# A verdict moved into the last products, and a linear attention plus gated MLP kernel's order table written anew

## The chip, the cores and the metric

The kernel runs on one core of one Trainium2 chip. The metric is device time in microseconds (us) of one execution; less is better. The core has five engines with a queue of instructions each, and every queue is executed in its own order: PE (matrix products), DVE (vector), ACT (scalar), POOL (GpSimd) and SP, which here only issues DMA transfers. Each instruction may wait on semaphores that other engines or transfers raise.

## What is computed

First a linear attention with a decaying state, for 4 batches, 8 heads, 768 positions and head size 48, then a gated MLP on the 3072 tokens with 384 features and 1536 hidden features:

```python
for t in range(S):
    state = alpha[:, :, t, :, None] * state + np.einsum('bhd,bhe->bhde', k[:, :, t], v[:, :, t])
    y[:, :, t] = np.einsum('bhd,bhde->bhe', q[:, :, t], state)
...
x = np.ascontiguousarray(attn_out.transpose(0, 2, 1, 3)).reshape(B * S, H * D)
g = x @ w_gate
silu = g * (1.0 / (1.0 + np.exp(-g)))
val = x @ w_val
return (silu * val @ w_out).astype(np.float32)
```

q, k, v and alpha are float32; the three weights come as 64-bit floats, and the kernel cuts their bits down to 32 itself.

## The kernel before

**Attention.** The positions of all batches are cut into 16 units u of 192. For each unit DVE makes two scans over the decays (`backward`, line 459, and `forward`, line 468), and q and k are multiplied by the results. PE makes the scores (`scores`, line 553), the state that is carried on (`carry`, lines 593 and 603) and the outputs (`outputs`, lines 658 to 675); DVE masks the scores (`causal`, line 613). The output rows are split into a high and a low part (`rows_hi` on ACT, line 689; `rows_lo` on DVE, line 693) and stored as columns of `xT`. In units 0 to 3 the inputs are turned by PE: `widened` copies an input to a padded tile (line 402), `pe_transposed` turns it (line 414), and a copy takes it out of PSUM (line 833). Later units are turned by DVE (line 394).

**MLP.** Tokens are worked on in 8 blocks of 384, hidden features in 12 pieces of 128: 96 steps. A step s has a gate product g and a value product v (`product`, line 748, nine matmuls each, three split products for each third of the features), ACT's silu (line 756), DVE's product `hidden` (line 760), the split of the hidden tile into a high part (`hidden_hi`, ACT, line 764) and a low part (`hidden_lo`, line 769, on DVE or POOL), and the out product o (`out_product`, line 780, nine matmuls into three PSUM banks). At the end of a block `out_rows` (line 792) takes the three banks out and `out_store` (line 797) stores them. The first block can start once units 0 and 1 are through. The g and the v product have one PSUM bank each, so v of the next step waits until `hidden` has read the one before.

**Weights.** Twenty groups of one or two pieces are loaded while the first steps run; each is cut from 64 to 32 bits in three operations (lines 156 to 174) and split in two (lines 340 and 344), shared among ACT, DVE and POOL.

**Range checks.** The fast path is right only where the weights and alpha lie in fixed ranges. So all weights and alpha are loaded once more (`range_load`, `alpha_load`) into three buffers and checked on ACT (lines 316 to 318 for each of 36 weight pieces, lines 453 and 454 for each of 16 alpha pieces), which leaves sums in `viol` and `wviol`. At the very end these are reduced on DVE, compared and multiplied, PE sums over the partitions (line 954), DVE writes `flag` (line 955), every engine loads `flag` into a register (line 1106) and branches on it (line 1107): past the slow general path where all is in range.

**The order.** `ORDER` is a text of some 1500 words that fixes, by hand, the order of nearly all instructions. A word such as `v:G0` or `t:S5@01` names an engine (t PE, v DVE, s ACT, g POOL, y SP), a task, and for PE the PSUM banks by number. The program takes the words in turn, each engine gets its instructions in that order, and the framework adds the semaphores. What stands behind the loop over `ORDER`, the reduction of the checks among it, was placed by the framework's own scheduler:

```python
for word in ORDER.split():
    e, name = word.split(":")
    name, *banks = name.split("@")
    todo.pop(name)(engines[e], *(BANKS[int(x)] for x in "".join(banks)))
```

Names in `ORDER`: `La0 Lq0 Lk0` load a unit's inputs, `pa0` widens alpha of unit 0, `Ta0` turns it, `ea0` takes it out, `G0 f0` are the scans, `S0 Bw0 B4 Y0` scores, carry and outputs, `ma` the mask, `yh yl` the split of output rows, `R x` and `xr` the way into `xT`; `w4v0 w4v1 w4v2 w4a w4p` are the five operations on weight group 4; `g3 v3 sl3 h3 hh3 hl3 o3 ot3 os3` belong to step 3; `wr wc` and `Lc ck` are loads and checks of the ranges.

Of the kernel before, what the change touches and what calls it, by code (L numbers as in the profile page):

```python
# [46 lines left out]
y:La0 s:pa0 y:wl0 t:Ta0@73 y:La1 s:ea0 y:Lq0 s:pa1 y:Lk0 v:w0v0 v:w0v1 v:w0v2 v:G0 t:Ta1@50 s:pq0 s:w0a y:Lq1 y:Lk1  # L47
v:f0 s:pk0 t:Tq0@36 t:Tk0@47 g:z0 g:pq1 v:q0 v:mk0 s:pk1 s:ea1 s:qc0 y:La2 t:Tk1@30 s:ek1 t:K0.2@4 y:Lk2 s:kc0.2
t:K0.0@1 v:G1 y:V0 s:kc0.0 t:Tq1@36 y:wl1 s:pa2 t:S0@05 v:mk1 g:w0p t:K0.1@7 t:K1.1@4 s:cq1 s:vc0 y:wl3 y:Lq2 s:kc0.1
y:wl2 v:f1 v:ma0.1 s:w1v0 v:ma0.0 g:q1 s:w3v0 t:Ta2@26 s:qc1 s:ea2 t:Bw0@7 s:ad0.2 v:z1 v:ma0.2 v:w1v1 v:w3v1 v:w1v2  # L50
s:ad0.1 y:V1 s:kc1.1 v:G2 t:K1.2@5 t:S1@16 g:w1a t:K1.0@2 v:de1 v:ma1.1 v:ma1.0 v:ma1.2 t:Y0@70 v:f2 y:La3 s:kc1.0
v:w3v2 s:kc1.2 v:z2 y:wl6 s:pa3 t:Bw1@4 s:yh0.0 s:w2v0 g:w1p t:Ta3@56 y:wl4 s:vc1 v:yl0.0 s:ad1.1 s:yh0.1 g:pk2
t:Y1@23 g:pq2 v:w2v1 y:V2 s:ad1.2 v:w2v2 s:w4v0 s:yh1.0 t:Tk2@41 s:w2a s:yh1.1 v:yl0.1 t:R0.1@0 v:mk2 t:Tq2@74 v:q2
t:R0.0@1 t:K2.0@7 v:yl1.0 y:Lk3 t:R0.2@4 s:x0.0 s:ea3 v:yl1.1 g:w3a s:kc2.0 y:Lq3 s:x0.2 s:pq3 v:x0.1 y:wl9 t:K2.2@2
t:R1.2@5 t:R1.0@6 t:R1.1@0 v:de2 t:K2.1@4 s:x1.1 v:w4v1 s:x1.0 g:w3p y:wl5 g:pk3 y:wl14 y:V3 t:Tk3@13 y:wl10 s:x1.2
g:w2p t:Tq3@70 v:G3 v:ad0.0 t:g0 s:kc2.1 v:w4v2 v:f3 s:kc2.2 s:cq3 s:w6v0 t:v0 s:w5v0 s:vc2 t:S2@70 v:w5v1 y:wl7 s:qc2
t:Bw2@2 s:sl0 s:w4a y:wl13 v:w5v2 g:q3 t:g1 g:w4p s:ad2.1 v:ma2.2 v:h0 y:La4 v:ma2.0 s:sl1 s:ad2.2 s:w5a t:v1 v:mk3
v:ma2.1 y:wl8 t:K3.1@4 v:de3 t:K3.0@1 s:kc3.1 v:w6v1 s:kc3.0 t:Y2@27 y:wl11 y:Lk4 s:yh2.0 s:hh0 t:S3@41 g:hl0 s:w7v0
v:w5p v:w6v2 t:Bw3@3 t:g2 v:ma3.2 v:h1 s:yh2.1 s:hh1 v:yl2.0 v:ma3.1 v:w7v1 v:w7v2 y:wl12 g:qc3 s:sl2 s:w9v0 g:w6a
s:ad3.1 t:v2 s:vc3 v:hl1 s:w7a v:ma3.0 t:g3 s:sl3 v:yl2.1 t:o0 t:Y3@01 v:h2 v:w7p g:w6p s:w8v0 t:K3.2@2 s:w10v0 v:w9v1  # L60
v:w9v2 s:hh2 g:z3 v:w8v1 v:w8v2 s:w8a v:w10v1 s:yh3.0 t:v3 v:h3 t:g4 t:o1 y:xr2 v:yl3.0 v:w8p g:hl2 t:v4 s:w9a s:sl4
t:o2 s:hh3 v:w10v2 s:yh3.1 g:hl3 t:g5 v:yl3.1 v:h4 s:w11v0 t:o3 v:w9p t:v5 s:w10a g:w10p s:w12v0 v:tr4 s:hh4 v:w11v1
v:w11v2 s:sl5 v:h5 t:g6 v:w12v1 v:w12v2 s:w14v0 t:v6 g:hl4 s:hh5 v:tk4 t:o4 s:w11a g:w11p y:xr3 s:sl6 t:g7 v:h6 v:G4
s:hh6 s:kc3.2 s:w12a s:w13v0 t:v7 g:hl5 y:Lq4 s:sl7 v:mk4 y:wl16 t:o5 v:w12p v:h7 t:g8 v:f4 g:hl6 g:z4 s:sl8 t:v8 t:g9
v:w14v1 s:hh7 v:hl7 y:wl15 v:w14v2 v:h8 s:sl9 t:o6 v:ot6.2 v:tq4 s:ot6.0 y:wl18 t:v9 s:hh8 t:g10 v:h9 v:w13v1 g:hl8
s:w15v0 t:v10 v:w15v1 y:os6.0 v:q4 g:qc4 s:sl10 v:w15v2 s:ot6.1 t:g11 v:w13v2 y:La5 s:w13a t:o7 s:hh9 v:h10 y:os6.1
# [1072 lines left out]
```

## Time and profile before

| what | value |
|---|---|
| time, three executions | 564.78 us median (563.24 to 565.94) |
| time of the profiled execution | 563.72 us |
| span of its trace, first to last instruction | 562.0 us |
| granted TensorE clock over the span, mean | 0.993 |
| busy: DVE | 387.3 us (69%) |
| busy: ACT | 277.5 us (49%) |
| busy: POOL | 158.2 us (28%) |
| DMA | 77.64 MB, mean 138 GB/s |

The profiled execution lies 1.06 us below the median of the three. The span is shorter than the time by 1.72 us, which lie around the program. A row of a timeline gives the start in us from the span's start, the time of the group, the engine, the line, the operation, output and input tiles by name, the shape, the number of instructions, and in brackets how long the engine stood idle before it and what ended that.

### The profile page before, as it was taken

What the parts mean: (1) busy time and instruction counts of PE and PEld (TensorE: products, weight loads), DVE (VectorE), ACT (ScalarE), POOL (GpSimd) and SP (SyncE); (2) the same over time, 40 slices, a digit from 0 to 9 for tenths busy, and PEclk for the clock granted to TensorE, in tenths of its full rate; (3) what the DMA queues carried; (4) which work ended last, traced back from release to release, by engine and by line L of the source; (5) the groups of instructions that cost most, each with busy time, mean ns of one, the idle gap of its engine ahead of it and who ended that gap; (6) DMA issues with size and microseconds to landing.
All of it is one profiled execution on the core that took longest, in us unless ns stands there. A gap on an engine that the chain in (4) does not pass through costs nothing.

```text
span 562.0 us, 13554 instructions
## 1 busy us (share of the span) xinstructions
PE 538.6 (96%) x5398; PEld 522.4 (93%) x5398; DVE 387.3 (69%) x599; ACT 277.5 (49%) x616; POOL 158.2 (28%) x159
## 2 busy tenths in 40 slices
PE   4899999998999999999999999999999999999992
PEld 4789899998899999999999999999999999999992
DVE  7999999979997888879879887754683403121121
ACT  6987653443123213244562453556666464546452
...
GB/s 244 271 240 261 203 170 164 176 103 114 135 146 156 98 153 155 118 106 183 77 163 141 150 90 182 157 87 170 188 138 58 71 109 146 71 77 106 22 77 48
DMA packets 95366, 77.64 MB, mean 138 GB/s; under 512 B 32832, under 2 KB 92224, under 8 KB 95296
## 3 DMA queue, kind: packets, MB, share of 16 engines
...
HBM read 62.52 MB, written 5.90 MB: 122 GB/s over the span
## 4 chain that ended last, share of the span: by engine, by line
PE 84%; DVE 10%; issue 2%; ACT 1%; DMA 1%; POOL 0%; ACTq 0%; DVEq 0%
PE ops L780 26%; PE g L748 25%; PE v L748 25%; PE y L675 2%; PE A L603 2%; PE s L553 2%; DVE Gs L459 2%; PE y L658 1%; DVE t L164 1%; DVE t L174 1%; DVE X L613 1%; PE y L659 1%; DVE V L642 1%; DVE AT L468 1%; DMA Le<-in_alpha_dram 1%
## 5 line engine op out<-in xcount | busy, mean ns | idle before, releaser
L748 PE MATMUL v<-xT,w 128*128 128x384 f32 x864 | 166.6, 336 | 1.4 <-DVE h L760 1.4
L748 PE MATMUL g<-xT,w 128*128 128x384 f32 x864 | 166.8, 337 | 0.0
L780 PE MATMUL ops<-w,hh 128*128 128x384 f32 x576 | 160.9, 337 | 0.8 <-DVE X L613 0.8
L769 POOL TENSOR_TENSOR hl<-h,hh 128x384 fp32r<-128x384 f32 x63 | 74.2, 1179 | 291.2 <-ACT hh L764 291.1
L748 PEld LDWEIGHTS v<-xT,w 128*128 128x128 f32 x864 | 150.6, 188 | 2.6 <-DVE h L760 2.0
L748 PEld LDWEIGHTS g<-xT,w 128*128 128x128 f32 x864 | 150.4, 188 | 0.8
L760 DVE TENSOR_TENSOR h<-h,v 128x384 f32<-128x384 f32 x96 | 53.0, 552 | 112.6 <-PE v L748 97.1
L756 ACT ACTIVATE h<-g 128x384 f32<-128x384 f32 x96 | 47.0, 490 | 125.7 <-PE g L748 119.1
L780 PEld LDWEIGHTS ops<-w,hh 128*128 128x128 f32 x576 | 105.8, 188 | 1.7 <-DVE X L613 1.2
L780 PE MATMUL ops<-w,hl 128*128 128x384 f32 x288 | 96.9, 336 | 0.0
L764 ACT CAST hh<-h 128x384 fp32r<-128x384 f32 x96 | 48.8, 510 | 97.1 <-PE ops L780 60.3
L528 DVE STREAM_TRANSPOSE K<-Gs 32x384 f32<-32x384 f32 x96 | 54.7, 570 | 1.9
L780 PEld LDWEIGHTS ops<-w,hl 128*128 128x128 f32 x288 | 54.1, 188 | 0.0
L769 DVE TENSOR_TENSOR hl<-h,hh 128x384 fp32r<-128x384 f32 x33 | 21.5, 650 | 21.0 <-ACT hh L764 20.8
L468 DVE TENSOR_TENSOR_SCAN AT<-AT,back 128x771 f32<-128x771 f32 x16 | 29.5, 1846 | 0.6
L459 DVE TENSOR_TENSOR_SCAN Gs<-AT,inj 128x772 f32<-128x772 f32 x16 | 29.2, 1823 | 0.3 <-ACT AT L833 0.2
L613 DVE TENSOR_TENSOR X<-s,mask 64x384 f32<-64x384 f32 (+1 forms) x48 | 26.4, 552 | 2.0 <-PE s L553 1.2
L487 POOL TENSOR_TENSOR X<-trq,AT 112x768 f32<-112x768 f32 x10 | 17.9, 1786 | 35.2 <-DMA L<-in_k_dram 11.6
L344 POOL TENSOR_TENSOR w<-t,w 128x768 fp32r<-128x768 f32 (+1 forms) x14 | 25.5, 1824 | 3.7 <-ACT w L340 3.3
L174 DVE SCALAR_TENSOR_TENSOR t<-raw,t 128x768 uint32<-128x768 uint32 (+1 forms) x20 | 24.4, 1229 | 0.3
L317 ACT ACTIVATE wc<-wc,wbias 128x384 f32<-128x384 f32 x36 | 23.5, 653 | 1.2
L318 ACT ACTIVATE wc<-wc,wbias 128x384 f32<-128x384 f32 x36 | 23.4, 650 | 1.2
...
## 6 DMA issues: line engine op xcount, KB each, us to landing
...
```

The costliest lines, as they stand in the source:

```text
L174: eng.scalar_tensor_tensor(out=t, in0=hi, scalar=0x3FFFFFFF, in1=t, op0=ALU.bitwise_or, op1=ALU.bitwise_and)
L344: eng.tensor_tensor(out=lo, in0=src, in1=hi.bitcast(F32), op=ALU.subtract)
L459: nc.vector.tensor_tensor_scan(*(x.rearrange("p g t -> p (g t)")[:, ::-1] for x in (Gs, AT, inj)), 0.0, op0=ALU.mult, op1=ALU.add)
L468: nc.vector.tensor_tensor_scan(Af, Af, back[:, 1 : n + 1], back[:, 0:1], op0=ALU.mult, op1=ALU.add)
L528: nc.vector.transpose(out=bass.AP(k0.tensor, k0.offset, [k0.ap[0], (G * 2 * D, NU), (2 * D, G), (1, 32)]), in_=Kg[j * BO + x : j * BO + x ...
L613: nc.vector.tensor_tensor(out=X[r, z, f * GF : (f + 1) * GF, :].rearrange("r g (c t) -> r g c t", c=NU), in0=sps[f][r].rearrange("r g (c t ...
L748: nc.tensor.matmul(pt, wsp[kind, f][a][:, kt * P : (kt + 1) * P], xT[blk][:, b_, kt, :], start=(n == 0), stop=(n == 3 * KT - 1),)
L756: nc.scalar.activation(h, acc.pop(("g", blk, f)), AF.Silu)
L760: nc.vector.tensor_tensor(out=h, in0=h, in1=acc.pop(("v", blk, f)), op=ALU.mult)
L764: nc.scalar.copy(out=hh, in_=acc["h", blk, f])
L769: eng.tensor_tensor(out=hl, in0=acc.pop(("h", blk, f)), in1=hh.bitcast(F32), op=ALU.subtract)
L780: nc.tensor.matmul(ops[blk][i], h[b_][:, i * P : (i + 1) * P], wsp["o", f][a], start=(first and n == 0), stop=(last and n == 2),)
```

## The change

Three things are changed, and no arithmetic.

1. The reduction of the checks is no longer behind the loop. It is two tasks, `fa` (DVE: reduce, compare, multiply, and a memset of ones) and `fb` (PE's sum and DVE's write of `flag`), with places in `ORDER` among the last products.
2. `ORDER` is a new text: tasks stand elsewhere, some are on another engine, and PE's tasks have other banks. By count of tasks, 24 `hl` went from POOL to DVE and 22 from DVE to POOL, 4 q products went from DVE to POOL and 2 back, 3 k products from POOL to DVE and 1 back, 4 low weight parts from DVE to POOL and 3 back, 5 `ot` from ACT to DVE and 4 back. The widening of alpha of unit 0 goes from ACT to POOL.
3. The checks of the ranges are begun earlier and none is left for the end: 19 of 52 stand ahead of the gate product of step 48, where there were 8.

```diff
 ORDER = """
...
-t:o94 y:os83.1 t:o95 v:ot95.0 s:ck13 s:ot95.2 y:os95.0 v:ot95.1 y:os95.1 s:os95.2 v:z15 s:ck15
...
 """
...
+    checks = {}
+
+    def checks_joined(eng):
+
+        oks = []
+        for nm, t_, most in (("a", viol, 0.0), ("w", wviol[:, 0, :], 0.0), ("s", wviol[:, 1, :], W_SUM)):
+            vs = cp.tile([P, 1], F32, name="vs" + nm)
+            nc.vector.tensor_reduce(vs, t_, axis=AX.X, op=ALU.add)
+            okf = cp.tile([P, 1], F32, name="ok" + nm)
+            nc.vector.tensor_scalar(out=okf, in0=vs, scalar1=most, scalar2=None, op0=ALU.is_le)
+            oks.append(okf)
+        okf = oks[0]
+        for t_ in oks[1:]:
+            nc.vector.tensor_tensor(out=okf, in0=okf, in1=t_, op=ALU.mult)
+        ones = cp.tile([P, 1], F32, name="ones")
+        nc.vector.memset(ones, 1.0)
+        checks.update(ones=ones, okf=okf)
+
+    def verdict(eng):
+
+        cps = ps.tile([1, 1], F32, tag="A2", name="cps")
+        nc.tensor.matmul(cps, checks["ones"], checks["okf"], start=True, stop=True)
+        nc.vector.tensor_copy(out=flag, in_=cps)
+
+    todo["fa"] = checks_joined
+    todo["fb"] = verdict
...
-    oks = []
-    for nm, t_, most in (("a", viol, 0.0), ("w", wviol[:, 0, :], 0.0), ("s", wviol[:, 1, :], W_SUM)):
...
-    ones = cp.tile([P, 1], F32, name="ones")
-    nc.vector.memset(ones, 1.0)
-    cps = ps.tile([1, 1], F32, tag="A2", name="cps")
-    nc.tensor.matmul(cps, ones, okf, start=True, stop=True)
-    nc.vector.tensor_copy(out=flag, in_=cps)
```

The end of the new text reads `v:fa v:h95 t:o93 t:fb g:hl94 s:hh95 v:hl95 t:o94 y:os83.2 t:o95 s:ot95.0 s:ot95.1 s:ot95.2 y:os95.0 s:os95.2 y:os95.1`. The table shows little by itself; three places show what it makes of the queues. Line numbers of the changed kernel are lower by 89, since the text of `ORDER` has fewer lines.

**The end, on ACT and DVE.** `ac` is a piece of alpha under check, `ot` an output tile, `hh` a high part, `vs` and `ok` the sums and verdicts of the checks. ACT's last rows before:

```order
L764 CAST hh_11_6734<-h_11_6697 128x384
L453 ACTIVATE ac_6730<-ac_6730,nbias 128x576
L454 ACTIVATE ac_6730,viol<-ac_6730,dbias 128x576
L792 COPY ot_2_11_6763<-ops_2_0_6389 128x384
L797 DMA out_dram<-ot_2_11_6763 128x384
L453 ACTIVATE ac_6695<-ac_6695,nbias 128x576
L454 ACTIVATE ac_6695,viol<-ac_6695,dbias 128x576
L1106 TENSOR_LOAD flag
```

and now:

```order
L675 CAST hh_11_6760<-h_11_6725 128x384
L703 COPY ot_0_11_6783<-ops_0_0_6386 128x384
L703 COPY ot_1_11_6785<-ops_1_0_6387 128x384
L703 COPY ot_2_11_6787<-ops_2_0_6388 128x384
L708 DMA out_dram<-ot_2_11_6787 128x384
L1027 TENSOR_LOAD flag
```

DVE's last rows before:

```order
L769 TENSOR_TENSOR hl_11_6738<-h_11_6697,hh_11_6734 128x384
L792 COPY ot_0_11_6759<-ops_0_0_6387 128x384
L792 COPY ot_1_11_6766<-ops_1_0_6388 128x384
L472 MEMSET AT 128x3
L944 TENSOR_REDUCE vsa<-viol 128x1
L946 TENSOR_SCALAR oka<-vsa 128x1
L950 TENSOR_TENSOR oka<-oka,okw 128x1
L950 TENSOR_TENSOR oka<-oka,oks 128x1
L955 CAST flag<-cps 1x1
L1106 TENSOR_LOAD flag
```

Ahead of these, elsewhere on DVE, the scheduler had put the two sums over the weights, `vsw` and `vss`. Now:

```order
L671 TENSOR_TENSOR h_10_6700<-h_10_6700,v_10_6683 128x384
L850 TENSOR_REDUCE vsa<-viol 128x1
L852 TENSOR_SCALAR oka<-vsa 128x1
L850 TENSOR_REDUCE vsw<-wviol 128x1
L852 TENSOR_SCALAR okw<-vsw 128x1
L850 TENSOR_REDUCE vss<-wviol 128x1
L852 TENSOR_SCALAR oks<-vss 128x1
L856 TENSOR_TENSOR oka<-oka,okw 128x1
L856 TENSOR_TENSOR oka<-oka,oks 128x1
L858 MEMSET ones 128x1
L671 TENSOR_TENSOR h_11_6725<-h_11_6725,v_11_6713 128x384
L865 CAST flag<-cps 1x1
```

Two alpha checks leave ACT's end, the three output copies are all on ACT now, and the write of `flag` stands ahead of DVE's last `hl`, which is one row further on, followed by the load of `flag`. On PE the sum `cps` stands between the out products of steps 93 and 94. On SP the load of `flag` stands ahead of its last two stores.

**The beginning, on POOL and DVE.** `wide` is the padded tile for PE's turning, `Le` alpha of unit 0, `sel` and `K` constants, `raw` and `t` a weight piece before and after it is cut. POOL before:

```order
L242 AFFINE_SELECT mask<-mask 64x64 x2
L266 COPY K_105<-ident 48x4x48 x2
L371 CAST sel_121<-ident 48x48 x2
L371 CAST sel_122<-ident 48x48 x2
L472 MEMSET AT 128x3
```

and now:

```order
L153 AFFINE_SELECT mask<-mask 64x64 x2
L313 COPY wide<-Le 128x12x48
L177 COPY K_105<-ident 48x4x48 x2
L282 CAST sel_121<-ident 48x48 x2
L282 CAST sel_122<-ident 48x48 x2
L383 MEMSET AT 128x3
```

DVE before, from behind its memsets (a scan is printed as SCALAR_TENSOR_TENSOR with `Gs<-AT,inj` or `AT<-AT,back`):

```order
L158 TENSOR_SCALAR t_149<-raw_133 128x384
L168 SCALAR_TENSOR_TENSOR t_149<-raw_133,t_149 128x384
L174 SCALAR_TENSOR_TENSOR t_149<-raw_133,t_149 128x384
L459 SCALAR_TENSOR_TENSOR Gs_153<-AT,inj 128x772
L465 RECIPROCAL back<-Gs_153 128x4
L468 SCALAR_TENSOR_TENSOR AT<-AT,back 128x771
```

and now, from the second scan pair on (unit 0's pair comes first, with nothing ahead of it):

```order
L370 SCALAR_TENSOR_TENSOR Gs_202<-AT,inj 128x772
L773 TENSOR_TENSOR Gs_202<-trk_215,Gs_202 128x4x192
L376 RECIPROCAL back<-Gs_202 128x4
L379 SCALAR_TENSOR_TENSOR AT<-AT,back 128x771
L75 SCALAR_TENSOR_TENSOR t_186<-raw_172,t_186 128x384
L85 SCALAR_TENSOR_TENSOR t_186<-raw_172,t_186 128x384
L524 TENSOR_TENSOR X_103<-s_0_245,mask 128x384
```

The copy of alpha has come to POOL, and the cutting of the first weight piece has moved from ahead of unit 0's scans to behind unit 1's.

**Around unit 4's output rows, on DVE.** `X<-y` is `rows_lo`, which frees the banks that the scores of unit 5 (`S5@01`) take; `t<-raw` with 384 elements is the last weight group. Before:

```order
L394 STREAM_TRANSPOSE trq_1864<-L_72 128x4x6x32
L760 TENSOR_TENSOR h_9_1862<-h_9_1862,v_9_1844 128x384
L164 SCALAR_TENSOR_TENSOR t_1880<-raw_1841,t_1880 128x384
L174 SCALAR_TENSOR_TENSOR t_1880<-raw_1841,t_1880 128x384
L528 STREAM_TRANSPOSE K_105<-Gs_1659 32x12x32 x2
L394 STREAM_TRANSPOSE AT<-L_71 128x4x6x32
L693 TENSOR_TENSOR X_103<-y_4_1775,X_103 112x2x192
L693 TENSOR_TENSOR X_103<-y_4_1774,X_103 112x2x192
```

and now:

```order
L69 TENSOR_SCALAR t_1907<-raw_1846 128x384
L79 SCALAR_TENSOR_TENSOR t_1907<-raw_1846,t_1907 128x384
L680 TENSOR_TENSOR hl_9_1934<-h_9_1853,hh_9_1931 128x384
L604 TENSOR_TENSOR X_103<-y_4_1779,X_103 112x2x192
L671 TENSOR_TENSOR h_10_1910<-h_10_1910,v_10_1921 128x384
L439 STREAM_TRANSPOSE K_105<-Gs_1534 32x12x32 x2
L85 SCALAR_TENSOR_TENSOR t_1907<-raw_1846,t_1907 128x384
L604 TENSOR_TENSOR X_103<-y_4_1780,X_103 112x2x192
```

The first of the two `rows_lo`, the one that frees a bank of `S5@01`, has come ahead of the last operation on that weight group and of two of the K transposes; on PE, ten products stand between the outputs of unit 4 and the scores of unit 5, where there were eight.

More of the change, by code (lines that the diff above doesn't have):

```diff
@@ L46 @@
 ORDER = """
[L47 to L66, printed above, removed]
@@ L102 @@
-g:hl47 v:ma11.1 t:g49 t:o47 v:h48 y:xr10 s:sl49 v:kr12.1 t:v49 v:ma11.2 s:hh48 v:ma11.0 y:wr8 t:Y11@21 s:ot47.1
-s:ot47.0 t:g50 s:yh11.0 y:os47.1 v:h49 v:kr12.2 t:v50 g:z12 s:hh49 v:hl48 s:yh11.1 v:yl11.0 v:hl49 v:kr12.3 y:Lk13
-s:sl50 v:ot47.2 t:g51 t:o48 v:q12 v:tr13 v:h50 s:sl51 s:wc7 t:g52 s:hh50 y:wr5 v:yl11.1 y:xr11 t:o49 t:v51 g:vc12
-y:Lq13 v:tk13 t:S12@01 v:hl50 s:wc5 v:G13 t:B12@2 y:V13 v:ma12.2 v:mk13 s:sl52 t:o50 s:ad12.0 v:h51 v:ad12.1 v:kr13.2
-t:g53 v:ma12.1 g:qc12 s:hh51 g:hl51 t:v52 s:sl53 v:ad12.2 t:o51 v:h52 v:ma12.0 t:g54 s:hh52 t:v53 t:Y12@12 v:hl52
@@ L107 @@
-v:tq13 v:h53 s:wc8 t:v54 v:kr13.1 s:hh53 g:hl53 v:kr13.0 s:sl54 y:wr12 y:La14 v:h54 t:o52 v:de13 v:f13 t:g55 v:z13
-t:v55 s:hh54 s:sl55 v:h55 t:o53 t:v56 g:hl54 g:q13 v:kr13.3 s:yh12.0 s:yh12.1 t:g56 v:yl12.0 v:tr14 y:wr16 s:wc16
-y:wr20 s:hh55 t:o54 t:S13@01 v:yl12.1 s:sl56 v:h56 t:B13@2 v:G14 s:hh56 t:g57 v:ad13.0 s:wc12 g:hl56 s:sl57 y:Lk14
-t:v57 v:hl55 t:o55 v:ad13.1 v:f14 v:h57 y:os47.2 y:Lq14 v:ma13.2 v:ad13.2 t:g58 y:os47.0 y:wr11 t:v58 g:qc13 s:wc11
-g:vc13 v:ma13.1 v:ma13.0 s:sl58 y:wr22 t:Y13@01 s:hh57 g:hl57 v:h58 s:wc20 t:v59 y:wr17 s:yh13.0 v:yl13.0 s:yh13.1
@@ L939, in main_path @@
             todo.pop(name)(engines[e], *(BANKS[int(x)] for x in "".join(banks)))
-    oks = []
-    for nm, t_, most in (("a", viol, 0.0), ("w", wviol[:, 0, :], 0.0), ("s", wviol[:, 1, :], W_SUM)):
-        vs = cp.tile([P, 1], F32, name="vs" + nm)
-        nc.vector.tensor_reduce(vs, t_, axis=AX.X, op=ALU.add)
-        okf = cp.tile([P, 1], F32, name="ok" + nm)
-        nc.vector.tensor_scalar(out=okf, in0=vs, scalar1=most, scalar2=None, op0=ALU.is_le)
-        oks.append(okf)
-    okf = oks[0]
-    for t_ in oks[1:]:
-        nc.vector.tensor_tensor(out=okf, in0=okf, in1=t_, op=ALU.mult)
-    ones = cp.tile([P, 1], F32, name="ones")
-    nc.vector.memset(ones, 1.0)
-    cps = ps.tile([1, 1], F32, tag="A2", name="cps")
-    nc.tensor.matmul(cps, ones, okf, start=True, stop=True)
-    nc.vector.tensor_copy(out=flag, in_=cps)
 @with_exitstack
```

60 lines of the change are left out of this document (1 added, 59 removed).

## The prediction

> **What bounds the kernel now.** I read the page first, then PE's busy time by stretches, then PE's idle times one by one, then the end of the span.
>
> ```profile
> span 562.0 us, 13554 instructions
> PE 538.6 (96%) x5398; PEld 522.4 (93%) x5398; DVE 387.3 (69%) x599; ACT 277.5 (49%) x616; POOL 158.2 (28%) x159
> 7.40:36.00 28.60, 25.29 (x465) 21.52 (x466) 27.78 (x40) 24.80 (x60) 14.00 (x14) 1.00 0.93 253
> 120.00:150.00 30.00, 27.34 (x302) 26.28 (x301) 28.56 (x41) 11.03 (x22) 14.96 (x11) 1.00 0.46 120
> 150.00:551.60 401.60, 401.50 (x3775) 393.15 (x3773) 246.91 (x406) 187.66 (x434) 77.67 (x77) 1.00 0.47 121
> ```
>
> In a row of a stretch stand its length, then busy time and instructions of PE, weight loads, DVE, ACT and POOL, the granted clock, and DMA. From 150 to 551.6 PE has no gap: 401.50 of 401.60. The change takes no matmul away, so there is nothing to win there. What can move is the opening (in 7.4 to 36 DVE is busy for 27.78 of 28.60 and sets the pace), PE's single waits up to 150, and what lies behind the last product.
>
> **The end.** Rows of the timeline, then the branch and what follows it:
>
> ```profile
> 551.17 0.34 PE L780 MATMUL ops<-w,hh 128*128 128x384 f32 x1
> 551.54 0.48 ACT L792 COPY ot<-ops 128x384 f32<-128x384 f32 x1 [1.02 <-PE ops L780]
> 552.05 0.38 ACTq L797 DMA_DIRECT2D out_dram<-ot  x1
> 552.48 0.78 ACT L453 ACTIVATE ac<-ac,nbias 128x576 f32<-128x576 f32 x1 [0.45 <-ACT ot L792]
> 553.28 0.77 ACT L454 ACTIVATE ac<-ac,dbias 128x576 f32<-128x576 f32 x1
> 555.30 0.14 DVE L955 CAST flag<-cps 1x1 int32<-1x1 f32 x1 [0.37 <-PE cps L954]
> L1106 ACTq TENSOR_LOAD <-flag x1: 472/472/472, 555.5 to 555.5; - x1
> L1107 PEldq COMPARE_BRANCH  x1: 3842/3842/3842, 556.1 to 556.1; - x1
> L1107 SPq EVENT_SEMAPHORE  x8: 17/17/17, 559.4 to 560.0; - x8
> L1106 SPq FUSED_REGOPS  x1: 187/187/187, 560.0 to 560.0; - x1
> L1134 SPq EVENT_SEMAPHORE  x10: 17/28/28, 560.4 to 562.0; - x10
> ```
>
> The last product ends at 551.51. ACT stores the last tile, then still checks a piece of alpha (552.48 to 554.16); DVE, PE and DVE again make the flag of it (to 555.44); all engines load it (0.47), branch at 556.0, and none goes on before 559.4. The span ends at 562.0: 10.5 us behind the last product.
>
> Now nothing stands between ACT's last store and the load of the flag, which has long been written. With E the end of the last product: ACT's third copy runs to E + 0.51 (the first two run beside the last six matmuls, 0.48 each against 0.52 of PE), the store's issue to E + 0.92, the load to E + 1.45. From the branch to the end it took 562.0 - 556.0 = 6.0; SP's register work (0.19, with what follows it 0.35) now lies ahead, and SP itself branches a microsecond before ACT, so ACT's way alone counts: about 4.8 from its branch. E + 6.3 against E + 10.5: **4.2 us less**. Bounds: 3.0 less, if all 6.0 follow ACT's branch; 4.8 less, if PE's own load and branch (0.49 + 3.84) and the barrier of about 1.05 are what remains. The added sum on PE is the same pair of small matmuls, now at 0.2 us in PE's line. DVE has about nine small operations of 0.15 to 0.19 between h94 and h95: 1.5 us, beside g95, v95 and o93, which take PE 4.7.
>
> The Trainium skill (Runtime: NRT & Kernel Launch, Instruction fetch mechanics) says that a taken branch whose target is outside the loaded window waits for a fetch of its page by DMA. The trace agrees: PE's branch took 3.84 us, and nobody goes on before 559.4. By this rule the early flag can't hide the fetch, and that term stays in the end as I have it; if it could, the end would be 3.4 us shorter still.
>
> **The opening.** Rows of the timeline before:
>
> ```profile
> 4.31 0.67 ACT L402 COPY wide<-Le 128x576 f32<-128x576 f32 x1 [2.21 <-DMA Le<-in_alpha_dram]
> 4.82 0.52 POOL L242 TENSOR_SCALAR_AFFINE_SELECT mask<-mask 64x64 f32<-64x64 f32 x2
> 5.13 1.51 PE L414 MATMUL pt<-ident,wide 128*128 128x128 f32 x6 [5.13 <-ACT wide L402]
> 5.97 0.58 DVE L168 SCALAR_TENSOR_TENSOR t<-raw,t 128x384 uint32<-128x384 uint32 x1
> 7.39 1.77 DVE L459 TENSOR_TENSOR_SCAN Gs<-AT,inj 128x772 f32<-128x772 f32 x1 [0.24 <-ACT AT L833]
> 18.38 1.69 POOL L487 TENSOR_TENSOR X<-trq,AT 112x768 f32<-112x768 f32 x1 [4.78 <-DMA raw<-in_moe_w_out_dram]
> 32.22 1.04 DVE L859 TENSOR_TENSOR Gs<-pt,Gs 128x384 f32<-128x384 f32 x2 [0.19 <-PE pt L414]
> 34.17 1.01 DVE L693 TENSOR_TENSOR Y<-y,Y 112x384 fp32r<-112x384 f32 x2
> 36.44 0.57 PE L512 MATMUL kps<-ident,Gs 112*64 112x112 f32 x4
> 36.85 1.48 PE L414 MATMUL pt<-ident,wide 128*128 128x128 f32 x12
> 38.09 1.82 PE L748 MATMUL g<-xT,w 128*128 128x384 f32 x9
> ```
>
> Alpha's first copy ran on ACT to 4.98. POOL gets to it after its masks, at 5.34, and needs 0.7: PE turns alpha 1.0 us later, and DVE's first scan starts at about 8.4 instead of 7.39. Behind it DVE has no idle time to hide that. Its queue up to the output rows of unit 1 (the second of the two at 34.17 ends at 35.18) gets two cuts of the first weight piece that had filled the wait for the first scan (2 x 0.58, the row at 5.97) and one copy of a weight piece (not in these rows; taken like a cut of the same size, 0.55), and loses unit 2's k product (1.04 at 32.22), which moves behind the rows: 1.16 + 0.55 - 1.04 = 0.7. Rounded down to 0.6, for the cuts fill small gaps, these rows end 1.0 + 0.6 = 1.6 later.
>
> From there to PE's first product it was 38.09 - 35.18 = 2.9. Now a product v0 comes first; ahead of it stand more turnings of K (like the four at 36.44, 0.57 together, but each taken at its distance to the next task, together 0.4) and one turning of q less (half of the row at 36.85, 0.74): 2.9 + 0.4 = 3.3. First product at 35.2 + 1.6 + 3.3 = 40.1, 2.0 later. The turning of q that was done before 38.09 follows later, 0.74 of PE's own time. **The opening costs 2.7 us.** Bounds: 0, if POOL blocks DVE less here than it did (below), and 4.4, if its q product (1.69, the row at 18.38) blocks DVE once more.
>
> **The single waits.** PE's idle times behind the first product, and what stood behind the largest:
>
> ```profile
> 46.64 1.84 PE L748 MATMUL v<-xT,w 128*128 128x384 f32 x9 [0.33 <-DVE h L760]
> 59.06 0.44 PE L780 MATMUL ops<-w,hh 128*128 128x384 f32 x1 [0.83 <-DVE X L613]
> 138.65 0.93 PE L553 MATMUL s<-X,Gs 48*64 48x64 f32 x48 [1.58 <-DVE X L693]
> 145.05 1.83 PE L748 MATMUL v<-xT,w 128*128 128x384 f32 x9 [1.08 <-DVE h L760]
> ...
> 130.13 2.04 POOL L487 TENSOR_TENSOR X<-trq,AT 112x768 f32<-112x768 f32 x1
> 130.63 4.73 DVE L174 SCALAR_TENSOR_TENSOR t<-raw,t 128x384 uint32<-128x384 uint32 x1
> 132.13 1.02 POOL L769 TENSOR_TENSOR hl<-h,hh 128x384 fp32r<-128x384 f32 x1
> 133.10 1.84 POOL L344 TENSOR_TENSOR w<-t,w 128x768 fp32r<-128x768 f32 x1
> ```
>
> Together 3.8 us. One DVE operation, of a size that took 0.58 at 5.97, took 4.73 while three POOL operations ran without a gap (130.13 to 134.94); DVE came 4.2 us late to the rows that free a PSUM bank of S5, and PE stood 1.58 there and 1.08 soon after. In the new order the first of these rows stands ahead of that weight operation, and ten products instead of eight cover S5. With PE itself some 2 us later the first two waits (0.33 and 0.83, both for a late DVE) shrink as well, as far as DVE is not later by the same. I take 1.0 of the 3.8 to be left: **2.8 us less**. Bounds: 3.8 less, and 4.2 more, if one such block (4.2) falls on a spot with no cover and the old waits stay.
>
> The Trainium skill (SBUF — State Buffer, Who interferes with whom) says that a DVE instruction with two SBUF inputs and a POOL instruction that reads SBUF exclude each other for a whole instruction, and that order of issue decides. The trace agrees at 130.63. The rule speaks against this change at one place: the two cuts now follow the second scan pair directly, while POOL is released by the same scan to a q product like the one at 18.38; before, masks stood there. By the rule the opening would be up to 1.7 us longer, 4.4; without it, 2.7.
>
> **Sum.** -4.2 + 2.7 - 2.8 = -4.3 us. Span 562.0 - 4.3 = 557.7; with the 1.72 around it 559.4, against 563.72 of the profiled execution. The median of the runs is 1.06 higher, so 560.5 for a median.
>
> **Rivals.** Each as a time for the median (564.78 now).
>
> *POOL blocks DVE elsewhere.* Of DVE's work much stays two-input, and POOL has as many tasks as before. One run of three POOL operations at a spot without cover costs the 4.2 of the block at 130.63 in full; with the 1.0 that I leave of the waits that is 4.2 + 1.0 - 3.8 = +1.4 in place of -2.8: -4.2 + 2.7 + 1.4 = -0.1, 564.7. For it: all four waits above name DVE, which is full in the opening; against it: 401 us without a gap behind 150.
>
> *The verdict holds PE.* `fb` stands in PE's line behind o93. If the last check on ACT ends only with o93, DVE's 1.5 us stand uncovered ahead of o94: -4.3 + 1.5 = -2.8, 562.0. For it: the check is two operations in the queue that also carries silu; against it: PE has 4.7 us of products in front, three times the 1.5.
>
> *The end doesn't shrink.* If the branch waits for something else than the flag (the slowest fetch, the stores' landing), only the check goes, and -4.2 becomes about -0.2: -0.2 + 2.7 - 2.8 = -0.3, 564.5. For it: 3.4 us of the end are not work but a fetch. Against it: the last store lands 2.0 us after its issue at 552.05,
>
> ```profile
> out_dram<-ot ACTq DMA_DIRECT2D x1, 192.0 KB, 2.0
> ```
>
> well ahead of 559.4, and the branch at 556.0 follows the load of the flag by half a microsecond.
>
> *The checks hold the products: slower.* A weight check is these rows, the second kind twice (L318 and a like one), and two short reads:
>
> ```profile
> L316 ACT ACTIVATE wc<-wc 128x384 f32<-128x384 f32 x36 | 19.8, 551 | 0.0
> L318 ACT ACTIVATE wc<-wc,wbias 128x384 f32<-128x384 f32 x36 | 23.4, 650 | 1.2
> 113.31 1.56 PE v L748 x9
> ```
>
> 2.2 us in ACT's queue ahead of a silu, of which the v product covers 1.56: 0.68 uncovered. 19 checks now stand ahead of step 48, where 8 stood, and in part of that stretch DVE and POOL still carry the attention. If all 19 cost 0.68, 12.9 us: -4.3 + 12.9 = +8.6, 573.4. It makes the kernel slower from seven such checks on (4.8), by over 0.5% from eleven. Against it: in the order before, 36 of the 52 checks (36 pieces of the weights, 16 of alpha) stood behind step 60, beside the same products, and PE had no gap there.
>
> **How the numbers follow.** Forecast 0.66 (its own range 557 to 562.5), POOL's blocking 0.14, the verdict 0.06, the end 0.05, the checks 0.09. A measurement of this kernel can tell about 0.5% (2.8 us) from no change, so faster by more ends at 562.0. Faster: the forecast, 0.66 (the verdict's 562.0 is at the line and counted as no change); within: 0.14 + 0.06 + 0.05 = 0.25; slower: 0.09. The terms at their best (-4.8, 0, -3.8) give -8.6, 556.2; I add one for the spread of the runs: low 555.0. Upwards the range takes in POOL's blocking, the verdict and the end: 565.0. What is left out is the checks' case and tails, under 2 in 10.
>
> **What would show it.** The end: from the last product to the end of the span 6.3 us (5.7 to 7.5), no `ac` or `vs` row behind the last product, the load of the flag on ACT 0.5 behind its last store. The opening: DVE's first scan at 8.4, PE's first product at 40.1. The waits: no idle of a microsecond ahead of S5, PE gapless from about 60 on; its last product ends at about 551.4. Wrong it would be made by a DVE row of several microseconds beside gapless POOL rows, or by PE rows that wait for ACT's silu in the steps up to 48.

## The result, and the profile after

The changed kernel took 556.4 us (median of four executions, 556.0 to 557.85) against 564.72 for the one before; the ratio is 0.9859 with a 95% interval of 0.9841 to 0.9878. It is faster by 8.3 us. The forecast was 560.5 (4.2 less) with a range of 555 to 565: the direction and all three places were right, and the gain was twice the one forecast.

The page of the profiled execution (556.0 us) begins so:

```profile
span 554.5 us, 13556 instructions
PE 537.3 (97%) x5398; PEld 523.1 (94%) x5398; DVE 379.8 (69%) x597; ACT 272.6 (49%) x606; POOL 152.7 (28%) x170
```

The span splits at two points, PE's first product and the end of its last one. These are rows by stretches, each from the first product to the end of the last; the first row is of the kernel before, the second of the changed one. Behind the length stands PE's busy time:

```profile
38.09:551.51 513.42, 509.59 (x4911) 497.85 (x4908) 352.27 (x540) 244.18 (x542) 137.36 (x120) 1.00 0.51 132
```

```profile
39.42:548.84 509.42, 509.42 (x4919) 498.46 (x4917) 347.02 (x549) 243.67 (x541) 136.68 (x128) 1.00 0.51 133
```

| part of the span | before | changed | difference | forecast |
|---|---|---|---|---|
| to the first product | 38.09 | 39.42 | +1.33 | +2.0 |
| first to last product: PE busy | 509.59 | 509.42 | -0.17 | +0.7 |
| first to last product: PE idle | 3.83 | 0.00 | -3.83 | -2.8 |
| from the last product to the end | 10.5 | 5.6 | -4.9 | -4.2 |
| span | 562.0 | 554.5 | -7.5 | -4.3 |

**The end**, in the changed kernel. First rows of its timeline, then of the load of the flag and the branch by engine (duration, then first and last start):

```profile
545.53 0.15 DVE L865 CAST flag<-cps 1x1 int32<-1x1 f32 x1 [1.07 <-PE cps L864]
548.50 0.34 PE L691 MATMUL ops<-w,hh 128*128 128x384 f32 x1
549.44 0.38 ACTq L708 DMA_DIRECT2D out_dram<-ot  x1
L1027 ACTq TENSOR_LOAD <-flag x1: 692/692/692, 549.9 to 549.9; - x1
L1028 DVEq COMPARE_BRANCH  x1: 72/72/72, 546.6 to 546.6; - x1
L1028 PEldq COMPARE_BRANCH  x1: 3342/3342/3342, 547.2 to 547.2; - x1
L1028 SPq COMPARE_BRANCH  x1: 45/45/45, 549.6 to 549.6; - x1
L1028 ACTq COMPARE_BRANCH  x1: 54/54/54, 550.6 to 550.6; - x1
L1028 SPq EVENT_SEMAPHORE  x8: 17/17/17, 552.4 to 552.9; - x8
L1028 ACTq EVENT_SEMAPHORE  x1: 17/17/17, 553.4 to 553.4; - x1
L1055 SPq DRAIN  x3: 7/7/13, 553.5 to 553.8; - x3
```

The flag is there 3.2 us ahead of the end of the last product (548.84). DVE and PE branch while PE still works on its matrix products: the 3.34 us of PE's branch run from 547.2 to 550.5, half of them beside the products. Two engines branch behind the last product: SP, which stores two of the three parts of the last tile, at 549.6, and ACT, which copies all three and stores one, at 550.6. Both go on 2.8 later. SP then runs sixteen semaphore instructions (the eight at 552.4 to 552.9, and eight like them) and reaches the closing barrier at 553.56, ACT at 553.49; the barrier ends at 554.5.

**The waits.** PE has no idle time at all behind 39.42. Where it stood 1.58 us ahead of S5, rows of POOL and DVE now read:

```profile
130.84 2.32 DVE L439 STREAM_TRANSPOSE K<-Gs 32x384 f32<-32x384 f32 x4
133.20 0.67 DVE L69 TENSOR_SCALAR t<-raw 128x384 uint32<-128x384 uint32 x1
133.90 0.56 DVE L79 SCALAR_TENSOR_TENSOR t<-raw,t 128x384 uint32<-128x384 uint32 x1
134.85 0.55 DVE L604 TENSOR_TENSOR X<-y,X 112x384 fp32r<-112x384 f32 x1
```

```profile
130.00 3.65 POOL L255 TENSOR_TENSOR w<-t,w 128x768 fp32r<-128x768 f32 x2 [0.29 <-ACT w L251]
```

POOL again runs for 3.65 us without a gap, but what stands beside it on DVE are four transposes with one input (0.58 each, their usual time). The first operation from there on with both inputs in SBUF, at 133.90, comes when POOL has ended, and takes 0.56.

**The opening.** POOL widens alpha at 5.41, DVE's first scan starts at 8.29:

```profile
5.41 0.66 POOL L313 COPY wide<-Le 128x576 f32<-128x576 f32 x1
8.29 1.77 DVE L370 TENSOR_TENSOR_SCAN Gs<-AT,inj 128x772 f32<-128x772 f32 x1 [4.25 <-ACT AT L744]
19.22 1.68 POOL L398 TENSOR_TENSOR X<-trq,AT 112x768 f32<-112x768 f32 x1 [5.33 <-ACT trq L744]
19.38 1.94 DVE L85 SCALAR_TENSOR_TENSOR t<-raw,t 128x384 uint32<-128x384 uint32 x1
28.58 0.29 PE L504 MATMUL s<-V,K 128*48 128x48 f32 x2 [1.49 <-DVE X L524]
39.42 1.81 PE L659 MATMUL v<-xT,w 128*128 128x384 f32 x9
```

The second cut of the first weight piece, 19.38, took 1.94 instead of 0.56 beside POOL's q product. That is the collision by which the prediction let the opening reach its upper bound; yet the first product came 1.3 later, not 3.7 (2.0 and 1.7).

### The profile page after: what moved, and what is told of

The parts are those of the page before. It is cut to its first block, busy times and chain, and to the rows that moved or that the text cites. A ratio compares the mean times of both kernels' runs of the same rounds, so it can differ in the third digit from the quotient of the medians.

```text
span 554.5 us, 13556 instructions
## 1 busy us (share of the span) xinstructions
PE 537.3 (97%) x5398; PEld 523.1 (94%) x5398; DVE 379.8 (69%) x597; ACT 272.6 (49%) x606; POOL 152.7 (28%) x170
## 4 chain that ended last, share of the span: by engine, by line
PE 94%; DVE 3%; POOL 1%; issue 1%; ACT 0%; DVEq 0%; POOLq 0%; ACTq 0%
PE ops L691 27%; PE g L659 27%; PE v L659 27%; PE s L464 2%; PE y L586 2%; PE A L514 2%; PE y L569 1%; PE y L570 1%; PE pt L325 1%; PE A L504 1%; DVE AT L379 1%; DVE Gs L370 1%; DVE X L524 1%; PE kps L423 0%; PE xp L626 0%
## 5 line engine op out<-in xcount | busy, mean ns | idle before, releaser
L680 POOL TENSOR_TENSOR hl<-h,hh 128x384 fp32r<-128x384 f32 x61 | 71.2, 1167 | 278.3 <-ACT hh L675 260.3
L680 DVE TENSOR_TENSOR hl<-h,hh 128x384 fp32r<-128x384 f32 x35 | 19.9, 571 | 18.9 <-ACT hh L675 18.7
L398 POOL TENSOR_TENSOR X<-trq,AT 112x768 f32<-112x768 f32 x12 | 21.2, 1764 | 32.4 <-DVE trq L305 10.7
L325 PE MATMUL pt<-ident,wide 128*128 128x128 f32 x72 | 13.4, 341 | 8.3 <-POOL wide L313 6.1
```

The costliest lines, as they stand in the source:

```text
L680: eng.tensor_tensor(out=hl, in0=acc.pop(("h", blk, f)), in1=hh.bitcast(F32), op=ALU.subtract)
```

## The experiments

Three questions were open: whether the verdict's place alone makes the end shorter and whether it can cost something elsewhere; whether the one DVE operation of 4.73 us was the cause of PE's waits; and what sets the opening. Kernels that begin with `b_` are the one before with a few words of `ORDER` moved, those with `a_` the changed one. "First" and "length" are PE's first product and the time from it to the end of the last, "end" what follows; the times are medians, each beside the kernel before on the same chip.

| kernel | time | before | ratio (95%) | first | length, idle in it | end |
|---|---|---|---|---|---|---|
| b_verdict | 564.75 | 564.22 | 1.0004 (0.9987 to 1.002) | 39.11 | 516.69, 6.1 | 6.3 |
| b_verdict_spread | 562.75 | 564.95 | 0.9964 (0.9949 to 0.9978) | 39.54 | 514.98, 4.5 | 6.6 |
| b_q5_later | 561.55 | 564.22 | 0.9957 (0.9936 to 0.9979) | 38.27 | 510.17, 1.0 | 10.8 |
| b_q5_order | 563.77 | 564.95 | 0.9982 (0.9967 to 0.9997) | 39.13 | 512.52, 3.0 | 10.7 |
| b_cut_later | 561.38 | 563.90 | 0.9957 (0.9939 to 0.9975) | 37.97 | 510.20, 0.9 | 10.3 |
| b_both | 561.95 | 564.95 | 0.9947 (0.9927 to 0.9966) | 40.74 | 514.43, 4.0 | 6.7 |
| a_verdict_last | 558.21 | 564.22 | 0.989 (0.9866 to 0.9915) | 39.45 | 509.70, 0.2 | 8.4 |
| a_masks_first | 557.12 | 564.22 | 0.9873 (0.985 to 0.9896) | 39.45 | 509.69, 0.2 | 6.6 |
| a_v1_early | 557.97 | 563.90 | 0.9885 (0.9864 to 0.9906) | 40.28 | 509.29, 0.0 | 6.7 |
| a_v1_masks_store | 557.90 | 563.90 | 0.9895 (0.9874 to 0.9916) | 39.34 | 509.71, 0.2 | 7.4 |
| a_open | 556.05 | 564.14 | 0.9859 (0.9842 to 0.9875) | 37.55 | 510.00, 0.0 | 6.1 |
| changed, again | 557.35 | 564.95 | 0.9867 (0.9847 to 0.9888) | 39.41 | 509.68, 0.1 | 7.0 |

### The verdict's place

The first kernel has the two new tasks, and the last six checks drawn ahead:

```diff
-... y:wr35 ... s:ck11 ... s:wc35 ... s:ck14 ... s:ck10 ... s:ck13 ... s:ck15
+... y:wr35 ... s:ck6 s:ck11 y:Lc10 y:Lc14 ... s:hh89 s:wc35 y:Lc15 ... s:hh90 s:ck10 y:Lc13 ... s:hh91 s:ck14 ... s:hh92 s:ck15 ... s:hh93 s:ck13
-... v:h95 t:o93 ... v:hl94 v:hl95
+... v:fa v:h95 t:o93 t:fb ... v:hl94 v:hl95
```

> The kernel before with the verdict alone moved: the last six checks are drawn ahead, the reduction stands before h95 and PE's sum and the write of the flag behind o93; nothing else of the order is changed. If the end is worth what the two traces show (10.5 us behind the last product before, 5.7 after), the time falls by about 4.8 us from 564.7 to about 560, with PE's last product still ending at 551 to 552. Rival: the changed kernel's end is short because its three output copies are all on ACT and not because of the verdict; then 10.5 stays within 2 us of itself, 563 or more. Rival: the checks drawn ahead hold PE in the last steps; then PE's idle time behind 450 us is over 1 us.

The end fell to 6.3, and yet the time did not move. PE's length had grown by 3.3, of which the rows of its idle time name 2.4:

```profile
532.73 1.83 PE L748 MATMUL g<-xT,w 128*128 128x384 f32 x9 [2.09 <-ACT h L756]
552.58 0.44 PE L780 MATMUL ops<-w,hl 128*128 128x384 f32 x1 [0.34 <-DVE hl L769]
```

The short end rules out the first rival, since two of the three output copies are on DVE here. The first wait is the other rival: four checks stood on ACT between the silu at 524.3 and the next one at 532.2, two of them in a row, where the order before had one. The second wait is one that the prediction did not have: DVE's write of the flag waits for PE's sum behind o93, hl94 stood behind that write in DVE's queue, and o94 needs hl94.

```profile
551.91 0.15 DVE L954 CAST flag<-cps 1x1 int32<-1x1 f32 x1 [1.07 <-PE cps L953]
551.99 1.00 DVE L769 TENSOR_TENSOR hl<-h,hh 128x384 fp32r<-128x384 f32 x2
```

In the changed kernel hl94 is on POOL, which takes it out of this queue. The mended kernel spreads the last thirteen checks over the steps 85 to 94, one at a time, and does the same with hl94:

```diff
-s:hh94 ... v:hl94
+s:hh94 g:hl94
```

> As the first kernel with the verdict alone, mended at the two places where that one lost what the end won: the last thirteen checks stand one at a time between ACT's tasks of the steps 85 to 94 instead of three in a row, and hl94 is on POOL, as in the changed kernel, so that it no longer stands behind DVE's write of the flag. If those two places were the whole loss, PE has no idle time behind 450 us, the end is 6 to 6.5 us as in the first one (6.3), and the time is 4 to 4.5 us below the kernel before: about 560. If moving the verdict is worth nothing as such, it stays at 564.

The end is 6.6, and o94 no longer waits. Two new waits of 0.54 and 0.44 us remain besides the old ones (at 507.9 and 522.8), both behind a check on ACT: in the second PE waits for a low part whose high part stood behind the check, in the first for a hidden product that stood on DVE behind such a low part. It is faster by 0.4%, half of what was expected; the first product came 1.5 later than in the profile before, of which more below. The reverse leaves the checks early in the changed kernel and puts the verdict back:

```diff
-v:fa v:h95 t:o93 t:fb g:hl94 s:hh95 v:hl95 t:o94 y:os83.2 t:o95 ...
+v:h95 t:o93 g:hl94 s:hh95 v:hl95 v:fa t:o94 y:os83.2 t:o95 t:fb ...
```

> The changed kernel with the reduction of the checks behind hl95 and PE's sum behind o95, checks as early as they are. All engines then load the flag behind the last product and branch together. If the early flag as such is what the end gains, the end grows from 5.7 by the flag's chain (0.4), the load (0.5) and a branch that takes PE's 3.8 again: to about 7 us, 557.7 for a median. If the check of alpha that stood at the end was the whole gain, it stays at 5.7, 556.4. If the early loads on the other engines are the whole gain, it goes back to over 9, 560.

The end is 8.4, between the first answer (about 7) and the third (over 9). All engines branch within 0.6 us, and now each is slow to go on:

```profile
L1028 PEldq COMPARE_BRANCH  x1: 3698/3698/3698, 550.2 to 550.2; - x1
L1028 SPq COMPARE_BRANCH  x1: 45/45/45, 550.5 to 550.5; - x1
L1028 ACTq COMPARE_BRANCH  x1: 54/54/54, 550.7 to 550.7; - x1
L1028 SPq EVENT_SEMAPHORE  x8: 17/17/17, 554.5 to 555.1; - x8
L1028 ACTq EVENT_SEMAPHORE  x1: 17/17/17, 554.7 to 554.7; - x1
```

From its branch ACT took 4.0 us to go on, against 2.8 and 3.2 in two profiles of the changed kernel. Of the 4.2 between the old and the new end, this kernel keeps about half; that half is what drawing the checks ahead is worth, and an early flag is worth the rest, as far as one profile tells.

### The operation of 4.73 us

```diff
-s:yh4.1 v:w19v2 g:q5 t:g17 v:kr5.0 y:Lk6 y:os13.1 g:hl16 t:v17 v:tr6 v:yl4.1 y:pl18.1 s:sl17 v:yl4.0 g:w18p
+s:yh4.1 v:w19v2 t:g17 v:kr5.0 y:Lk6 y:os13.1 g:hl16 t:v17 v:tr6 v:yl4.1 y:pl18.1 s:sl17 v:yl4.0 g:w18p g:q5
```

> The kernel before with one POOL instruction moved: the q product of unit 5 stands behind the low part of weight group 18 instead of two tasks ahead of it. DVE's order is the same. If the three POOL operations without a gap made the cut at 130.63 take 4.73 us, it now takes 1 us or less, the idle time of 1.58 before S5 goes and that of 1.08 before v19 goes or shrinks: 2 to 2.7 us less, 562.0 to 562.7. Rival: DVE is late there because it is full; then PE waits as before, 564.7. Rival: the block moves to the next two-input operation behind; then one DVE operation near 134 to 137 takes over 2 us and PE waits there.

In this kernel q of unit 5 is multiplied by the decays of unit 6, since `tr6` writes them over unit 5's; its times alone are read. POOL was idle when the cut came, and the cut took 0.56:

```profile
130.58 0.56 DVE L174 SCALAR_TENSOR_TENSOR t<-raw,t 128x384 uint32<-128x384 uint32 x1
133.81 1.05 DVE L693 TENSOR_TENSOR X<-y,X 112x384 fp32r<-112x384 f32 x2
```

Both waits are gone and PE's length is 3.25 shorter. With the order of the decays kept (`g:hl16 g:w18p g:q5` where `g:q5` stood, ahead of `tr6`) it came out differently:

> The kernel before with POOL's q product of unit 5 behind hl16 and the low part of weight group 18, all three put ahead of the turning of unit 6's alpha on DVE, so that the decays it reads are its own. DVE's order is the same. By the block: the cut at 130.6 takes about 0.6 instead of 4.7, the waits of 1.58 and 1.08 are gone, PE needs 3 us less from its first product to its last, 561.5. By a DVE that is merely full: no change, 564.2.

The cut was short here too, and PE waited all the same:

```profile
131.35 0.56 DVE L174 SCALAR_TENSOR_TENSOR t<-raw,t 128x384 uint32<-128x384 uint32 x1
136.69 1.59 DVE L394 STREAM_TRANSPOSE AT<-L 128x768 f32<-128x768 f32 x1 [3.59 <-POOL X L487]
```

`tr6` may overwrite the decays only when POOL's q product has read them, and that one now ends at 136.65. A dependency took the place of the block, with most of its price (1.02 and 1.07 us of PE for 1.58 and 1.08), and neither theory had it. So the third kernel leaves POOL alone and moves the cut:

```diff
-v:w19v2 g:q5 ... v:yl4.0 g:w18p t:o15 v:h17
+g:q5 ... v:yl4.0 g:w18p t:o15 v:h17 v:w19v2
```

> The kernel before with the last cut of weight group 19 (the operation that took 4.73 us) behind h17 on DVE instead of ahead of unit 4's output rows; POOL's order and every dependency on the decays are as before. If the block of that one operation by POOL made S5 and v19 wait, the rows end at about 134 instead of 139, both waits go, and PE needs 2.7 us less from its first product to its last: 510.7 instead of 513.4, a time 2 to 3 us below the kernel before. If DVE is merely full, PE waits for it there all the same. If the block only moves, the cut takes over 2 us behind h17 and G6 or the next hidden product is late.

```profile
131.87 1.65 DVE L394 STREAM_TRANSPOSE AT<-L 128x768 f32<-128x768 f32 x1 [0.42 <-POOL X L487]
133.34 1.02 DVE L693 TENSOR_TENSOR X<-y,X 112x384 fp32r<-112x384 f32 x2
134.74 0.54 DVE L174 SCALAR_TENSOR_TENSOR t<-raw,t 128x384 uint32<-128x384 uint32 x1
```

The rows end 4.6 earlier than before, both waits are gone, PE's length is 3.2 shorter and the kernel 0.43% faster (0.25 to 0.61). POOL's three operations run as before, from 129.80 to 134.61, and the cut behind them takes 0.54. One word of the table, moved, is worth 2.5 us.

> The kernel before with these two edits together and nothing else of the new order. If the verdict's place and the one block are what the change wins, the two add up: 4.2 + 3 less, 557 of 564.2, within 1 us of the changed kernel in the same call. If the rest of the new order (the opening, the later checks, the other 40 tasks on other engines) carries part of the gain, it stays 2 us or more above the changed kernel.

Its second edit is that of b_q5_order, with the dependency, and it stays 4.6 us above the changed kernel measured beside it. In the profile: 1.3 by a later first product, 4.0 by idle time of PE (the old waits, and the two of the spread checks), 0.8 by PE's busy time, and nearly the same end. The later first product is not the order's alone: from 19.94 to 23.35 PE's granted clock was 0.50 in this profile. So the kernel does not tell whether two edits alone would do. b_verdict_spread and b_cut_later by themselves lie 2.2 and 2.5 us below the kernel before, together 4.7 of the 7.6 to 8.3.

> The changed kernel once more, beside the others of this call: 556 to 557. Its end was 5.6 us in its first profile and 6.6 in the kernel that differs from it in the opening alone; if the length of the instruction fetch behind the branch changes from one execution to the next, it lies between 5.5 and 7 again, and PE from its first product to its last at 509.4 to 509.8.

First product and length repeat to 0.3 us; the end was 7.0 instead of 5.6. ACT's time from branch to going on was 3.2 instead of 2.8, and SP's 3.9 instead of 2.8:

```profile
L1028 SPq COMPARE_BRANCH  x1: 45/45/45, 550.0 to 550.0; - x1
L1028 ACTq EVENT_SEMAPHORE  x1: 17/17/17, 554.1 to 554.1; - x1
L1055 SPq DRAIN  x3: 7/7/13, 555.1 to 555.4; - x3
```

ACT reaches the closing barrier at 554.2 here, but SP, with its sixteen semaphore instructions, only at 555.1. SP set this end.

### The opening

```diff
-t:S0@10 v:w0v1 t:Tq1@76 ... v:ad0.0 v:w0v2 ... v:ma0.2 v:ma0.1 v:ma0.0 s:pa2
+t:S0@10 t:Tq1@76 ... v:ad0.0 ... v:ma0.2 v:ma0.1 v:ma0.0 v:w0v1 v:w0v2 s:pa2
```

> The changed kernel with the two cuts of the first weight piece behind unit 0's masks on DVE instead of ahead of them, so that they no longer stand beside POOL's q product. If that product is what made the second cut 1.94 us long, it falls to about 0.56 and DVE's queue is 1.4 us shorter up to the output rows of unit 1; PE's first product at about 38.0 instead of 39.4, 555.0. Rival: another path sets the first product (the turned K, the weights); then it stays at 39.4 and the time at 556.4.

The cut fell to 0.56, and nothing was won, as the rival had it. DVE waits instead:

```profile
20.79 1.14 DVE L524 TENSOR_TENSOR X<-s,mask 64x384 f32<-64x384 f32 x2 [1.46 <-ACT SE L545]
22.55 0.56 DVE L85 SCALAR_TENSOR_TENSOR t<-raw,t 128x384 uint32<-128x384 uint32 x1
28.61 0.29 PE L504 MATMUL s<-V,K 128*48 128x48 f32 x2 [1.83 <-DMA V<-in_v_dram]
```

The last two masks of unit 0 cannot start before 20.79; the cuts had filled most of that gap, and the block with them. The last row named the load of v as what PE waited for at 28.61, so the next kernel had `y:V1` right behind `y:V0`.

> The changed kernel with the loads of unit 1's v (six, on SP) directly behind those of unit 0 instead of behind two loads for unit 2. In five runs PE began the sums over unit 1's v at 28.58 to 28.61 whether DVE was ready or not, and its first product at 39.41 to 39.46. If the landing of v sets that, they begin up to 1.5 us earlier and the first product comes at about 38; the time falls by about 1.4 us against the changed kernel (556.4 to 557.4). If DVE sets it, the start stays at 28.5 and the first product at 39.4. Third: alpha and q of unit 2, now 3 us later, hold unit 2's scan; then the first product stays and PE waits behind it.

The sums still begin at 28.56, and the first product came 0.9 later. ACT now waited for alpha of unit 2, but that was made up for by 24.5. What is left is PE's clock: for 3.41 us the column of the granted clock, third from the end of its row, reads 0.50, where the changed kernel has 1.00. PE's outputs of unit 0 ran to 28.3 instead of 26.8, and the work behind them came late:

```profile
21.75 0.67 ACT L313 COPY wide<-L 128x576 f32<-128x576 f32 x1 [0.48 <-DMA L<-in_alpha_dram]
24.26:27.67 3.41, 3.41 (x53) 2.91 (x54) 3.33 (x8) 2.79 (x6) 0.47 (x1) 0.50 0.91 322
27.95 0.56 DVE L524 TENSOR_TENSOR X<-s,mask 64x384 f32<-64x384 f32 x1
```

The last row is what PE waits for in truth: unit 1's last mask ends at 28.5 to 28.6, here as in the changed kernel, a_masks_first and the next one. In the row of the kernel ahead the name of the wait was wrong: by the trace the last of unit 1's six loads had landed at 21.9.

> The same with two more words moved: the two cuts behind unit 0's masks (no block by POOL's q product, 1.4 us of DVE), and the last store on SP instead of ACT. If v and the block bound the opening together, the first product comes at 37.5 to 38 and the time falls by 1.5 to 2 us against the changed kernel. The end: ACT branches 0.4 to 0.5 earlier, so 6.0 instead of 6.4 on average; if SP's branch, now behind three stores, is as late as ACT's was, nothing. Rival: the opening stays at 39.4.

Nothing was won at either end. The first product came at 39.34: with the same loads and the clock at 1.00 throughout the opening it is where a_masks_first had it (39.45), so neither v of unit 1 nor alpha of unit 2 sets it. ACT branched at 550.0 and SP at 550.2, nearly together, and took 4.0 and 3.7 us to go on: what the earlier branch won was lost behind it.

So DVE's queue had to be shortened where it does not wait. The last kernel has the start of the one before:

```diff
-y:La0 g:pa0 y:Lq0 ... v:G0 ... y:wl0 ... s:w0v0 ... v:w0v1 ... v:w0v2
+y:La0 s:pa0 y:wl0 y:Lq0 ... v:w0v0 v:w0v1 v:w0v2 v:G0
```

> The changed kernel with the start of the one before: alpha of unit 0 widened on ACT, the first weight piece loaded second, and all three steps of its cutting on DVE ahead of the first scan; the rest of the new order stays. If DVE's queue from the first scan on sets the opening, the scan starts at 7.4 (8.4 where alpha lands a microsecond later) instead of 8.29, and the two cuts no longer stand between unit 1's scans and unit 0's masks: those masks end at 21.0 instead of 22.8, PE's first product comes at 37.6 instead of 39.4 (38.5 with a late alpha) and the time is 555 to 556 where the changed kernel took 556.4 to 557.4. If something else holds PE at 28.6 (v of unit 1, K of unit 1 on ACT), the first product stays at 39.4. The end and the waits behind the first product are those of the changed kernel.

```profile
7.45 1.76 DVE L370 TENSOR_TENSOR_SCAN Gs<-AT,inj 128x772 f32<-128x772 f32 x1 [0.32 <-ACT AT L744]
21.09 0.96 DVE L75 SCALAR_TENSOR_TENSOR t<-raw,t 128x768 uint32<-128x768 uint32 x1
37.55 1.84 PE L659 MATMUL v<-xT,w 128*128 128x384 f32 x9
```

The first product came at 37.55, as worked out from DVE's queue, 1.87 earlier than in the changed kernel, and its last one ends 1.3 earlier (547.55). The median is 556.05 against 556.4 and 557.35 of the changed kernel in its two measurements. The ratios overlap, so by time alone it is not shown to be faster; the trace shows where it is ahead.

## Why the prediction was right, and where its sizes were off

**What bounds the kernel** held: no gap behind 150 before, none behind 39.42 now. Everything that moved lies in the opening, in four waits and behind the last product.

**The end, forecast -4.2, right in size, but counted along another path.** In five profiles with the new end (the changed kernel twice, a_masks_first, a_v1_early, a_open) it was 5.6 to 7.0, mean 6.4; in four with the old one 10.3 to 10.8, mean 10.6. The forecast was 6.3. The profile of the result has a short one by chance (5.6), which makes -4.9 of it. The forecast let ACT's way alone count, with 4.8 us from its branch to the end; in the five profiles these were 3.8 to 5.2. But SP, which branches behind the last product too, reaches the closing barrier last in all fourteen profiles, in the five 0.07 to 0.93 us behind ACT. So it is partly chance that the sum fits so well. Its best bound, 4.8 less, does not follow from its terms either: 0.49 + 3.84 + 1.05 is 5.4, which is 5.1 less.

Two readings on the way were wrong. One is that all engines stand still until 559.4 in the trace before: POOL goes on at 556.2. The other is that the early flag cannot hide the fetch behind the branch. For PE it hides half of the branch beside the last products and the rest beside ACT's copy and store, and DVE is through at 549.5; only what ACT and SP do behind their late branches stays in the end. The rule of the Trainium skill that the sentence was drawn from (Runtime: NRT & Kernel Launch, Instruction fetch mechanics: a taken branch to a target outside the loaded window waits for the fetch of its page) agrees with the stalls in both traces; what was wrong is the conclusion that the stalls of all engines follow the last product. That the work of nine small DVE operations is covered was right. That `fb` could hold PE was a rival with one mechanism; b_verdict shows another, a queue: what stands on DVE behind the write of the flag waits for PE's sum too.

**The waits, forecast -2.8 of 3.8, too small.** All went. For the two largest the mechanism is shown: two edits of another kind (b_q5_later, b_cut_later) that keep the cut away from POOL remove both. That the new order wins them the same way is read from its trace; the two further products ahead of S5 were hardly needed, since both `rows_lo` are through at 138.9 there, S5 starts at 142.2, and the two take 3.1. In b_cut_later the first two waits stay (0.2 and 0.8 us), in the changed kernel they are gone; what removes those was not tried. The 1.0 that the forecast left over was not counted from any row.

**The opening, forecast +2.7, too large.** The forecast spreads it over the first two rows of the table above, and these came to +1.2 (+1.33 and -0.17): this is the term that was off most. In the two profiles the opening cost 1.33 to the first product and some 0.8 for the turning of q behind it, while PE's other work between the two products took about 1.0 less. The count for DVE was of the right kind: DVE's queue sets the first product, and the forecast for a_open that was made from it held to 0.05 us. But the two cuts stood in a gap in which DVE had to wait for the masks' scores anyway. In a_open the first product is 1.87 earlier, of which 0.84 is the earlier scan; so the cuts, their collision with POOL included, had cost 1.03, where the counts give 1.16 + 1.36. The copy of a weight piece, taken as 0.55, was 0.36. By the prediction's use of the rule of the Trainium skill (SBUF — State Buffer, Who interferes with whom) the opening was to be up to 1.7 longer; the trace agrees with the block itself (1.94 for 0.56), and a_masks_first, without it, is no faster: it stood in DVE's wait.

The other half of this error is that one execution of the kernel before was taken for all. Seven profiles of kernels with the old opening show the first product at 37.97, 38.09, 38.27, 39.11, 39.13, 39.54 and 40.74, mean 39.0; the changed one at 39.41, 39.42 and 39.45. Two of the reasons are shown. The 40.74 is that of b_both, with its 3.41 us at a clock of 0.50. And alpha's first copy on ACT starts when the load has landed, at 4.31 in the profile before, and in b_verdict a microsecond later, with everything behind it:

```profile
5.39 0.67 ACT L402 COPY wide<-Le 128x576 f32<-128x576 f32 x1 [3.29 <-DMA Le<-in_alpha_dram]
```

In the changed kernel POOL gets to that copy at 5.41 in any case, so an alpha as late as this would cost nothing there. Against the mean of the six at full clock, 38.7, the new opening costs 0.7 to the first product and not 1.3. Where the 39.13 and the 39.54 lost their time was not settled.

**What stays open.** PE's busy time between first and last product fell by 0.17, though it now holds the turning of q (0.8) and the sum for the flag. About 1 us of this is not assigned, the same that is missing in the opening's sum. That the whole change is these three things was not shown by a kernel either, since b_both had the wrong edit; it follows from the split of the span alone.

**The checks** ahead of step 48, the slower rival, cost nothing: PE has no gap there. b_verdict shows that the mechanism is real: four checks between two silus cost 2.1.
